# Turning the convolution's kernels onto time: TensorE transposes or transposing transfers

## The chip, the cores and the metric

The kernel runs on one core of one Trainium2 chip. The metric is the device time of one execution in microseconds (us): the median of three timed runs. Beside them stands one profiled execution, whose span runs from its first to its last instruction.

## The reference

Four layers are applied to `x` (2048 positions, 640 channels), each with a residual: attention, a convolution over positions, the same attention, the same convolution. Cut to what matters:

```python
def _A_ref(x, wqkv, wo):               # 32 heads of 20 channels
    q, k, v = split(x @ wqkv)
    return (softmax(q k^T * Dh ** -0.5) v) @ wo
def _B_ref(u, log_A_real, A_imag, C_real, C_imag, log_dt, D_skip):
    K = 2.0 * einsum("dn,dnl->dl", C, exp(A * dt * pos)).real    # one kernel of 2048 taps per channel
    y = irfft(rfft(K, 2 * L) * rfft(u^T, 2 * L), 2 * L)[:, :, :L]
    return y + u * D_skip
x = x + _A_ref(_layernorm(x), ...); x = x + _B_ref(_layernorm(x), ...)   # and both once more
```

## The kernel before, in words

During the first attention the kernels `K` (640 channels by 2048 taps) are computed beside it and stored in HBM as `kd`. They are needed as spectra. `ktransform` makes these from `kd` for both convolutions, once, while the first attention's output projection runs (`out_proj`). It takes the channels in five blocks of 128 (`b`). Each block goes through these steps:

- `load_kl(b)`: a 1 MB transfer on SP's queue brings `kl`, channels on partitions and 2048 taps along them.
- `by_time(b, h)`, two halves: TensorE turns eight groups of 128 taps (float32 transposes, four to one PSUM tile `pkt` of pool X). ScalarE writes the high float16 part `ktrh` (in the code `hi`) out of PSUM, scaled, and VectorE the low part `ktrl` (`lo`). The second half ends with `load_kl(b + 1)`.
- `first_stage(b, n)`, four of them: 24 float16 matmuls each with the constants `e1` on the parts, into two PSUM tiles `pkx` of pool X; ScalarE and VectorE copy one each to `x1` (in the trace `kx`).
- `turned(t, xt, h)`, four of them: 8 float32 transposes out of `x1` into two PSUM tiles `pkt` of pool X; one goes to `xt` by ScalarE and one by VectorE (`kxt`).
- `ends(t, xt, s, dst)`, four of them: 32 small matmuls `pkf`, four copies `kn`, two stores of 512 KB to `kha` or `khb`. It reads the whole of one `xt`.

`ktransform` is a generator. `out_proj` works through 16 rows of 30 matmuls each (`po`, 128x320 in float32 parts), 480 in all. It takes one step of the generator ahead of its first matmul and one more after every seven (`mm` and `weave`); what is left over runs after the last. Before the change there are 2 + 4 + 4 x 14 + 8 = 70 steps. `matmul` and `transpose` tie each matmul to the one before, so TensorE runs in just this order. Pool X has two PSUM tiles, pool M (for `po`) two, `kn` two per kind.

Each row of `out_proj` splits the row after next into parts: ScalarE writes `oh`, VectorE `ol`, of which there is one buffer; a transfer `otl` on SP's queue loads the next. After a row, the layer norm runs on VectorE and ScalarE (`u`, `uh`) and GpSimd (`ul`). SP issues its transfers in order: those of the constants (`e1s` first), of `otl`, `kl` and the stores of `kn`. The tile `late[1]` holds the last VectorE instruction of the attention; `hold` ties the first VectorE step of a block behind it, and later behind the last scaled copy of `turned`.

When `out_proj` is done, `ssm`, the convolution, begins with matmuls `psx` on `uh` and `ul`, and loads `eb` and the spectra `ka`, `kb`.

Of the kernel before, what the change touches and what calls it, by code (L numbers as in the profile page):

```python
# [11 lines left out]
F32 = mybir.dt.float32  # L12
F32R = mybir.dt.float32r
F16 = mybir.dt.float16
BF16 = mybir.dt.bfloat16
AF = mybir.ActivationFunctionType
ALU = mybir.AluOpType
# [4 lines left out]
P = 128  # L22
# [3 lines left out]
NCT = D // P  # L26
# [61 lines left out]
def mha_s4d_kernel(ctx, tc, x_in, wqkv, wo, lar, aim, cr, ci, ldt, dsk,  # L88
# [4 lines left out]
    def tie(made, before):  # L93

        if before is not None:
            tc.add_manual_dep(made.ins, before.name, mybir.DependencyInfo(
                mybir.DependencyClass.NoSync, mybir.DependencyReason.DATA), reason="order")
        return made.ins

    te = nc.tensor  # L100
    se, ve, ge, sy = (Ordered(e, plan, tie, e is nc.vector) for e in (nc.scalar, nc.vector, nc.gpsimd, nc.sync))
# [10 lines left out]
    def pst(pool, *a, **k):  # L112
        return ps_[pool].tile(*a, **k)
# [4 lines left out]
    kha = dram.tile([2 * NCT, P, 4, 4, P], F32, name="kha")  # L118
    khb = dram.tile([2 * NCT, P, 4, 4, P], F32, name="khb")
# [10 lines left out]
    ident = cp.tile([P, P], F32, name="ident")  # L130
# [5 lines left out]
    ksc = cp.tile([P, 2], F32, name="ksc")  # L136
# [52 lines left out]
    def chain(ins):  # L189
        last[0] = tie(ins, last[0])  # L190

    def matmul(*a, **k):
        chain(te.matmul(*a, **k))  # L193

    def transpose(*a, **k):
        chain(te.transpose(*a, **k))  # L196
# [1022 lines left out]
    def load_kl(b):  # L1219

        sy.dma_start(kl0[0], kd[b * P:b * P + P, :])
# [18 lines left out]
    def by_channel(x1, i2):  # L1240
        return x1[:, :, i2].rearrange("p c s g -> p s c g")

    def of_group(x1, g):
        return x1[:, :, :, :, g].rearrange("p c i s -> p (c i s)")

    def ktransform(e1):

        c = ExitStack()
        c2 = c.enter_context(tc.tile_pool(name="f2", bufs=2))
        kl, skip, f2, x1, hi, lo, *xts = kl0  # L1250
        hold = [late[1]]

        def by_time(b, h):

            if h == 0:
                tie(ve.tensor_add(kl[:, 0:1], kl[:, 0:1], skip[:, b:b + 1]), hold[0])
            klv = kl.rearrange("d (p i) -> d i p", i=NI)
            for i4 in (2 * h, 2 * h + 1):
                pt = pst("X", [P, 4, P], F32, tag="X", name="pkt")
                for i in range(4):  # L1260
                    transpose(pt[:, i, :], klv[:, 4 * i4 + i, :], ident)
                s4 = slice(4 * i4, 4 * i4 + 4)
                se.activation(hi[:, s4, :], pt, AF.Copy, scale=ksc[:, 0:1])
                ve.scalar_tensor_tensor(lo[:, s4, :], pt, ksc[:, 0:1], hi[:, s4, :], ALU.mult, ALU.subtract)
            if h and b + 1 < NCT:
                load_kl(b + 1)

        def first_stage(b, n):
            for i2 in (2 * n, 2 * n + 1):
                ps = pst("X", [P, 2, 2, P], F32, tag="X", name="pkx")  # L1270
                for i in range(2):
                    s = 2 * i2 + i
                    for r in range(2):
                        for n, (e, m) in enumerate(((0, hi), (0, lo), (1, hi))):
                            matmul(ps[:, r, i, :], e1[:, e, s, r, :], m[:, s, :], start=(n == 0), stop=(n == 2))
                (ve.tensor_copy if i2 % 2 else se.copy)(by_channel(x1, i2), ps.rearrange("p r i (c g) -> p (r i) c g", c=4))

        def block(b):

            def turned(t, xt, h):  # L1280
                for q in (2 * h, 2 * h + 1):
                    pt = pst("X", [P, 4, P], F32, tag="X", name="pkt")
                    for g in range(4):
                        transpose(pt[:, g, :], of_group(x1, 16 * t + 4 * q + g), ident)
                    if q % 2:
                        hold[0] = ve.tensor_scalar_mul(xt[:, q], pt, ksc[:, 1:2]).ins
                    else:
                        se.activation(xt[:, q], pt, AF.Copy, scale=ksc[:, 1:2])

            def ends(t, xt, s, dst):  # L1290
                px = [pst("F", [P, 512], F32, tag=f"F{ch}", name=f"pkf{ch}") for ch in range(4)]
                for ch in range(4):
                    rows = slice(32 * ch, 32 * ch + 32)
                    for g in range(4):
                        matmul(px[ch][32 * g:32 * g + 32, :].rearrange("p (q k) -> p q k", k=P), f2[rows, s, :],
                               xt[rows, :, g, :], start=True, stop=True, tile_position=(32 * ch, 32 * g))
                for h in range(2):
                    kn = c2.tile([P, 2, 4, P], F32, name=f"kn{s}")
                    for ch in range(2):
                        (se.copy if ch else ve.tensor_copy)(kn[:, ch], px[2 * h + ch].rearrange("p (q k) -> p q k", k=P))  # L1300
                    sy.dma_start(dst[2 * b + t][:, 2 * h:2 * h + 2], kn)
            steps = [(turned, 0, xts[0], 0), (turned, 0, xts[0], 1), (by_time, b + 1, 0), (ends, 0, xts[0], 0, kha),
                     (turned, 1, xts[1], 0), (ends, 0, xts[0], 1, khb), (turned, 1, xts[1], 1), (by_time, b + 1, 1),
                     (ends, 1, xts[1], 0, kha), (first_stage, b + 1, 0), (ends, 1, xts[1], 1, khb),
                     (first_stage, b + 1, 1), (first_stage, b + 1, 2), (first_stage, b + 1, 3)]
            for f, *a in steps:
                if f in (turned, ends) or b + 1 < NCT:
                    f(*a)
                    yield
        for h in range(2):  # L1310
            by_time(0, h)
            yield
        for n in range(4):
            first_stage(0, n)
            yield
        for b in range(NCT):
            yield from block(b)
        c.close()
# [329 lines left out]
    def seq(x, general):  # L1648

        stats = None  # L1650
        for n in range(0, len(parts), 2):
            with ExitStack() as c:
# [23 lines left out]
                with ExitStack() as c2:  # L1676
                    up2 = c2.enter_context(tc.tile_pool(name="up2", bufs=2 + n))

                    def ln(i0, m):
                        held = []  # L1680

                        def one(i):
                            if not held:
                                held.extend(ln_stats(lambda i: x[:, i0 + i, :], m))
                            mv, rs = held
                            ln_u(x, i0 + i, 1, (mv[:, i:i + 1, :], rs[:, i:i + 1]), uh, ul, up2, not general)
                        return [lambda i=i: one(i) for i in range(m)]
                    if general:
                        for i0 in range(0, NI, LG):
                            for f in ln(i0, LG):  # L1690
                                f()
                    else:
                        if n == 0:
                            filler[:] = ktransform(consts[0]), 0.0, False
                        out_proj(x, *tail, ln, load if early else None)
                        se.floor = None
# [97 lines left out]
```

## Time and profile before

| | |
|---|---|
| median of three runs | 2646.85 us (2645.38 to 2647.79) |
| span of the profiled execution | 2647.0 us |
| TensorE (PE) busy | 94% of the span |
| ScalarE (ACT) busy | 89% |
| VectorE (DVE) busy | 57% |
| GpSimd (POOL) busy | 30% |

The profile shows one execution. Its own time is its span, 2647.0 us; nothing around it is shown, and it stands 0.15 us from the median. The page gives busy times, but matmuls are pipelined, so the duration of one says less than the distance between the starts of two. The chain of waits follows the work back from the last instruction; there a group of matmuls appears with the time that it holds the chain.

### The profile page before, as it was taken

What the parts mean: (1) busy time and instruction counts of PE and PEld (TensorE: products, weight loads), DVE (VectorE), ACT (ScalarE), POOL (GpSimd) and SP (SyncE); (2) the same over time, 40 slices, a digit from 0 to 9 for tenths busy, and PEclk for the clock granted to TensorE, in tenths of its full rate; (3) what the DMA queues carried; (4) which work ended last, traced back from release to release, by engine and by line L of the source; (5) the groups of instructions that cost most, each with busy time, mean ns of one, the idle gap of its engine ahead of it and who ended that gap; (6) DMA issues with size and microseconds to landing.
All of it is one profiled execution on the core that took longest, in us unless ns stands there. A gap on an engine that the chain in (4) does not pass through costs nothing.

```text
span 2647.0 us, 118800 instructions
## 1 busy us (share of the span) xinstructions
PE 2492.4 (94%) x52388; PEld 1409.8 (53%) x52388; DVE 1519.5 (57%) x3430; ACT 2344.0 (89%) x2763; POOL 801.7 (30%) x1230
## 2 busy tenths in 40 slices
PE   6899999999999999899898999999999998999898
PEld 3444444454444444587896544454444443444898
DVE  7587777777765887577786323232232222143875
ACT  7899999999999999655665899999999999999574
POOL 1123333233323332111681122222222223222285
PEclk9999999999999999999999999999999999999999
DMA  6522222322222221654652111121121113222466
GB/s 206 189 53 77 68 74 62 82 65 63 61 54 59 53 63 38 234 206 163 213 173 64 47 53 50 51 60 45 45 66 39 50 34 87 71 66 61 137 190 184
DMA packets 188158, 241.99 MB, mean 91 GB/s; under 512 B 43504, under 2 KB 128816, under 8 KB 186224
## 3 DMA queue, kind: packets, MB, share of 16 engines
q1 hardware_dynamic: 151936, 188.28, 22.6%
q0 software_dynamic: 35696, 46.01, 7.4%
q8 instruction: 413, 6.77, 1.1%
q14 instruction: 113, 0.93, 0.1%
HBM read 158.16 MB, written 76.00 MB: 88 GB/s over the span
## 4 chain that ended last, share of the span: by engine, by line
ACT 59%; PE 20%; issue 10%; DVE 3%; DMA 2%; POOL 1%; SPq 0%; ACTq 0%; POOLq 0%; DVEq 0%
ACT pt L78 57%; PE psy L1430 3%; PE pa L903 2%; PE psv L1430 2%; PE po L193 2%; PE psx L1430 2%; PE S L868 2%; PE pst L1452 1%; PE pkx L193 1%; PE pv L586 1%; PE m L620 1%; PE pkt L196 1%; PE pq L773 1%; DMA kb<-khb 1%; DMA kop<-ks 1%
## 5 line engine op out<-in xcount | busy, mean ns | idle before, releaser
L78 ACT ACTIVATE pt<-S 128x1024 f32<-128x1024 f32 x2048 | 1927.7, 1033 | 27.9 <-PE S L868 15.5
L903 PE MATMUL pa<-pt,V 64*32 64x512 f32 x16384 | 1096.9, 589 | 1.4 <-DVE oc L78 1.4
L868 PE MATMUL S<-qop,kop 61*32 61x512 f16 x16384 | 877.2, 380 | 82.7 <-ACT pt L78 67.8
L868 PEld LDWEIGHTS <-kop 61*32 61x32 f16 x16384 | 366.9, 89 | 737.3 <-issue 619.2
L903 PEld LDWEIGHTS pa<-pt,V 64*32 64x32 f32 x16384 | 312.7, 106 | 72.0 <-issue 8.6
L78 POOL DMA_DIRECT2D dn<-oc x248 | 122.7, 501 | 574.2 <-DVE oc L78 574.1
L78 DVE TENSOR_SCALAR qc<-m 128x512 f32<-128x512 f32 (+1 forms) x68 | 46.8, 688 | 312.0 <-PE m L620 312.0
L78 POOL DMA_DIRECT2D db<-dn x248 | 125.4, 512 | 141.5 <-DMA dn<-dr 136.9
L78 POOL DMA_DIRECT2D ot<-oc x256 | 130.5, 517 | 88.4 <-DVE oc L78 55.5
L620 PE MATMUL m<-xl,wh 64*32 64x512 f16 x2560 | 143.8, 376 | 0.3 <-issue 0.3
L620 PE MATMUL m<-xh,wh 64*32 64x512 f16 x2560 | 144.1, 378 | 0.0
L620 PE MATMUL m<-xh,wl 64*32 64x512 f16 x2560 | 143.8, 377 | 0.0
L78 DVE COPY oc<-pa 128x512 f32<-128x512 f32 x64 | 44.2, 690 | 172.9 <-PE pa L903 168.9
L78 ACT COPY xt<-pst 128x1024 f16<-128x1024 f16 x80 | 81.3, 1016 | 60.8 <-PE pst L1452 60.8
L620 PEld LDWEIGHTS <-wh 64*32 64x32 f16 x5120 | 90.3, 93 | 73.3 <-issue 30.8
L78 POOL DMA_DIRECT2D dn<-dr x62 | 34.6, 558 | 287.3 <-DVE dr L78 248.6
L1480 POOL TENSOR_TENSOR kb<-t,kb 128x512 f32<-128x512 f32 x76 | 97.2, 1280 | 65.2 <-DVE t L78 40.8
L78 DVE TENSOR_SCALAR V<-m 128x160 f32<-128x160 f32 x64 | 20.7, 324 | 163.4 <-PE m L586 163.4
L78 DVE TENSOR_TENSOR kb<-ktab 128x512 f32<-128x512 f32 x160 | 106.2, 683 | 0.0
L586 PEld LDWEIGHTS <-xh 128*128 128x128 f16 x960 | 79.7, 98 | 46.7 <-issue 31.4
L1480 POOL TENSOR_TENSOR ka<-ka,kb 128x512 f32<-128x512 f32 x76 | 97.5, 1283 | 6.0
L337 PEld LDWEIGHTS m<-kb,ka 128*32 128x32 f32 x3840 | 60.8, 109 | 71.0 <-issue 52.4
(312 smaller groups left out, 3936.4 us busy)
## 6 DMA issues: line engine op xcount, KB each, us to landing
ka<-kha SPq DMA_DIRECT2D x80, 256.0 KB
kb<-khb SPq DMA_DIRECT2D x80, 256.0 KB
db<-dn POOLq DMA_DIRECT2D x248, 64.0 KB, 3.2
kop<-ks SPq DMA_DIRECT2D x176, 80.0 KB
kpw<-wd POOLq DMA_DIRECT2D x60, 192.0 KB, 3.9
qop<-qs SPq DMA_DIRECT2D x256, 40.0 KB
ot<-oc POOLq DMA_DIRECT2D x256, 40.0 KB, 3.0
kha<-kn SPq DMA_DIRECT2D x20, 512.0 KB
```

Source lines behind the costliest of these rows:

```text
L78: made = f(out, *a, **k)
L193: chain(te.matmul(*a, **k))
L196: chain(te.transpose(*a, **k))
L337: chain(te.matmul(ps[32 * j:32 * j + 32, c8, :], a[n][:, ch, :], b[n][:, dd, :], start=(n == 0), stop=(n == 2), tile_position=(0, 32 * j)))
L586: chain(te.matmul(ps[:, :n], a_[:, ct, sl], m[:, ct, :], start=(k == 0), stop=(k == 14)))
L620: chain(te.matmul(ps[r][32 * t:32 * t + 32, :], a_[rows, ct, 32 * u:32 * u + 32], m[rows, ct, 512 * v:512 * v + 512], start=(k == 0), stop ...
L773: te.matmul(pq, a_[:, ct, :], m[:, ct, sl], start=(n == 0), stop=(n == 14))
L868: chain(te.matmul(S[32 * t:32 * t + 32, 512 * r:512 * r + 512], kt_[rows, kc + 32 * t:kc + 32 * t + 32], qt[rows, :], start=True, stop=Tru ...
L903: chain(te.matmul(pa[r][32 * j:32 * j + 32, :], V[rows, kt, VP * h:VP * h + 32], pts[j // 2][rows, 512 * (j % 2):512 * (j % 2) + 512], sta ...
L1430: at("pe", te.matmul(*a, **k))
L1452: at("pe", te.transpose(pt[:, k, g, :], of_group(x1[k], 4 * q + g), id16))
L1480: at("pool", getattr(ge, f)(*a))
```

## The change

`by_time` no longer uses TensorE or PSUM. Out of `kl` as loaded it writes the two float16 parts with channels still on partitions, 1024 taps at a time: ScalarE the high part, VectorE the low part. They lie in `klp`, which is the memory of `xts[1]`, the second `kxt` tile, seen as float16. A new step `turn(b, h)` issues two transposing transfers on SP's queue, each of a 128x1024 float16 half (256 KB), from `klp` to `hi` and `lo`.

The order of steps is another too. `by_time` runs two blocks ahead, within `first_stage` of the next block, and `turn` one block ahead, at the start of a block. Neither counts as a step in a block. At the start, `by_time(0)`, `turn(0)`, `by_time(1)` and `first_stage(0)` run one after another. There are 4 + 2 + 4 + 4 x 12 + 8 = 66 steps.

```diff
         kl, skip, f2, x1, hi, lo, *xts = kl0
         hold = [late[1]]
+        spare = xts[1].rearrange("p a b k -> p (a b k)").bitcast(F16).rearrange("p (n i k) -> p n i k", n=2, k=P)
+        klp = [spare[:, n] for n in range(2)]
 
         def by_time(b, h):
 
             if h == 0:
                 tie(ve.tensor_add(kl[:, 0:1], kl[:, 0:1], skip[:, b:b + 1]), hold[0])
             klv = kl.rearrange("d (p i) -> d i p", i=NI)
-            for i4 in (2 * h, 2 * h + 1):
-                pt = pst("X", [P, 4, P], F32, tag="X", name="pkt")
-                for i in range(4):
-                    transpose(pt[:, i, :], klv[:, 4 * i4 + i, :], ident)
-                s4 = slice(4 * i4, 4 * i4 + 4)
-                se.activation(hi[:, s4, :], pt, AF.Copy, scale=ksc[:, 0:1])
-                ve.scalar_tensor_tensor(lo[:, s4, :], pt, ksc[:, 0:1], hi[:, s4, :], ALU.mult, ALU.subtract)
+            s8 = slice(8 * h, 8 * h + 8)
+            se.activation(klp[0][:, s8], klv[:, s8], AF.Copy, scale=ksc[:, 0:1])
+            ve.scalar_tensor_tensor(klp[1][:, s8], klv[:, s8], ksc[:, 0:1], klp[0][:, s8], ALU.mult, ALU.subtract)
             if h and b + 1 < NCT:
                 load_kl(b + 1)
+
+        def turn(b, h):
+
+            s8 = slice(8 * h, 8 * h + 8)
+            for a_, b_ in ((hi, klp[0]), (lo, klp[1])):
+                sy.dma_start_transpose(a_[:, s8], b_[:, s8].rearrange("d i p -> d (i p)"))
...
-            steps = [(turned, 0, xts[0], 0), (turned, 0, xts[0], 1), (by_time, b + 1, 0), (ends, 0, xts[0], 0, kha),
-                     (turned, 1, xts[1], 0), (ends, 0, xts[0], 1, khb), (turned, 1, xts[1], 1), (by_time, b + 1, 1),
-                     (ends, 1, xts[1], 0, kha), (first_stage, b + 1, 0), (ends, 1, xts[1], 1, khb),
-                     (first_stage, b + 1, 1), (first_stage, b + 1, 2), (first_stage, b + 1, 3)]
+            steps = [(turn, b + 1, 0), (turn, b + 1, 1), (turned, 0, xts[0], 0), (turned, 0, xts[0], 1),
+                     (ends, 0, xts[0], 0, kha), (turned, 1, xts[1], 0), (ends, 0, xts[0], 1, khb), (turned, 1, xts[1], 1),
+                     (ends, 1, xts[1], 0, kha), (first_stage, b + 1, 0), (ends, 1, xts[1], 1, khb), (by_time, b + 2, 0),
+                     (first_stage, b + 1, 1), (by_time, b + 2, 1), (first_stage, b + 1, 2), (first_stage, b + 1, 3)]
             for f, *a in steps:
-                if f in (turned, ends) or b + 1 < NCT:
+                if f in (turned, ends) or a[0] < NCT:
                     f(*a)
-                    yield
+                    if f is not turn and f is not by_time:
+                        yield
+        for f in (by_time, turn):
+            for h in range(2):
+                f(0, h)
+                yield
         for h in range(2):
-            by_time(0, h)
+            by_time(1, h)
             yield
```

## Rows read from the trace of the kernel before

**Rows 1.** The page: span, and busy us (share) xinstructions of each engine.
```profile
span 2647.0 us, 118800 instructions
PE 2492.4 (94%) x52388; PEld 1409.8 (53%) x52388; DVE 1519.5 (57%) x3430; ACT 2344.0 (89%) x2763; POOL 801.7 (30%) x1230
```
**Rows 2.** Windows: stretch, length, busy us (xinstructions) of PE, PEld, DVE, ACT, POOL; clock.
```profile
1089.00:1099.00 10.00, 5.99 (x44) 4.40 (x33) 9.30 (x14) 3.34 (x5) 2.52 (x5) 0.97 0.81 238
...
1142.00:1175.00 33.00, 32.66 (x387) 27.68 (x385) 24.43 (x50) 19.88 (x34) 5.65 (x4) 1.00 0.56 200
```
**Rows 3.** Groups of instructions, 1089 to 1262 us: busy, mean ns | idle before.
```profile
L78 DVE TENSOR_SCALAR kxt<-pkt,ksc 128x512 f32<-128x512 f32 x20 | 15.0, 748 | 7.6 <-PE pkt L196 7.5
L78 DVE SCALAR_TENSOR_TENSOR ktrl<-pkt,ksc,ktrh 128x512 f16<-128x512 f32 x20 | 14.5, 747 | 9.9 <-ACT ktrh L78 9.8
L78 DVE TENSOR_TENSOR ol<-otl,oh 128x640 fp32r<-128x640 f32 x15 | 12.2, 814 | 0.2
L78 ACT ACTIVATE ktrh<-pkt,ksc 128x512 f16<-128x512 f32 x20 | 13.1, 684 | 11.8 <-PE pkt L196 11.7
L196 PE MATMUL pkt<-ident,kl 128*128 128x128 f32 x80 | 12.2, 297 | 5.1 <-ACT kxt L78 3.5 <-issue 1.2 <-ACT oh L78 0.3
L78 ACT CAST uh<-u 128x640 f16<-128x640 f32 x15 | 10.7, 720 | 0.0
```
**Rows 4.** Timeline of PE around one group of transposes: start, us, instruction [idle before].
```profile
1147.58 1.14 PE L196 MATMUL pkt<-ident,kl 128*128 128x128 f32 x8 [0.34 <-ACT oh L78]
1148.48 1.12 PE L193 MATMUL po<-woh,ol 128*128 128x320 f32 x6
```
**Rows 5.** The chain that ended last, 1152 to 1157 us: start, us, what.
```profile
1152.91 1.03 PE po L193 x7
1153.94 1.07 PE pkf L193 x32
1155.01 1.23 PE po L193 x7
1156.24 0.89 PE pkt L196 x8
```
**Rows 6.** Timelines of PE and DVE at the start of the projection.
```profile
1091.70 1.58 PE L193 MATMUL po<-woh,ol 128*128 128x320 f32 x7
...
1099.02 0.26 PE L193 MATMUL pkx<-ktrh,e1s 128*128 128x128 f16 x1 [3.51 <-DVE ktrl L78]
...
1096.86 0.76 DVE L78 TENSOR_TENSOR ol<-otl,oh 128x640 fp32r<-128x640 f32 x1
```
**Rows 7.** Timeline of SP's queue at the start of the projection.
```profile
1089.72 2.62 SPq L78 DMA_DIRECT2D e1s<-in_c_e  x4
...
1094.80 0.38 SPq L78 DMA_DIRECT2D kl<-kd  x1
```
**Rows 8.** DMA: queue's packets, MB, share; traffic 1089 to 1262 us; one issue's landing.
```profile
q1 hardware_dynamic: 151936, 188.28, 22.6%
...
DMA packets 16675, 31.85 MB, mean 184 GB/s; under 512 B 1446, under 2 KB 10039, under 8 KB 16141
...
kd<-ko POOLq DMA_DIRECT2D x20, 256.0 KB, 3.3
```
**Rows 9.** Timelines of DVE and PE in the last block, where nothing parts the steps.
```profile
1245.43 0.75 DVE L78 TENSOR_SCALAR kxt<-pkt,ksc 128x512 f32<-128x512 f32 x1
...
1246.34 1.14 PE L193 MATMUL pkf<-kxt,f 32*32 32x512 f32 x32
```
**Rows 10.** Timeline of PE at the end of the projection, and one wait of PE.
```profile
1257.07 1.69 PE L193 MATMUL pkf<-kxt,f 32*32 32x512 f32 x32
...
1263.57 0.22 PE L1430 MATMUL psx<-uh,e1s 128*128 128x128 f16 x1 [2.03 <-DVE x L78]
...
PE psx L1430 <- DMA kb<-khb: 0.4, 1, 0.4
```
**Rows 11.** Waits of SP's queue, 1089 to 1262 us: us in total, times, longest.
```profile
SPq L78 <- DVE ol L78: 42.8, 10, 12.6
```

## The prediction, before the run

> **What bounds the kernel now.** I read the page first. Over the whole span TensorE is busy 94% and ScalarE 89% [rows 1], but the change touches only the output projection of the first attention, about 1089 to 1258 us, so these shares decide nothing. The windows come next. In a settled stretch of 33.00 us TensorE is busy 32.66, VectorE 24.43, ScalarE 19.88 [rows 2]; there TensorE is the bound, and work taken from it should shorten the stretch one for one. At the start it is not: in the ten microseconds from 1089 it is busy 5.99, VectorE 9.30. The grouped instructions then show the transposes of `kl`: 80 of them, 12.2 us busy, with 5.1 us of idle time right before them, 3.5 of it until ScalarE's `kxt` [rows 3]. As matmuls overlap, I price a group of eight by the distance of starts: from 1147.58 to the next `po` at 1148.48, 0.90 us [rows 4]. The chain shows the beat that the rest keeps: seven `po` take 1.03 us (0.147 each), an `ends` 1.07, the seven after it 1.23, a `turned` 0.89 [rows 5].
>
> **What the change removes from TensorE.** Ten groups of eight transposes go. The first two lie in the start, which is settled by itself below; the other eight are on TensorE's path: 8 x 0.90 = 7.2 us off. Of the idle time before them, the 1.2 us of "issue" goes with them. The 3.5 us until `kxt` I keep: ScalarE's copy was late there, and the next step, now `ends`, reads the same tile after the same seven `po`. What comes out of step with it is priced below.
>
> **ScalarE and VectorE.** Twenty `ktrh` of 0.684 and twenty `ktrl` of 0.747 us become ten each of twice the length, out of SBUF with a step of 64 bytes [rows 3]. No row has that shape. Scaled from 640 to 1024 elements, `uh` (0.720) gives 1.15 us and `ol` (0.814) 1.30; the pairs they replace cost 1.37 and 1.49. Were the step to double them, 10 x 1.15 and 10 x 1.30 us more would spread over some 150 us in which each engine has idle time [rows 2]. I take nothing for either, since TensorE's beat covers them; without that cover it is up to 1.2 us a half for whatever copy queues behind, `kx` or the adds of `po` first.
>
> **The start.** Before, the first `pkx` came at 1099.02, after 3.51 us of waiting for `ktrl` [rows 6], and by the order of steps 14 `po` lay ahead of it. Now it is the seventh step, and 42 lie ahead: 28 x 0.147 = 4.1 us of later work is done early. When can it start? `po` begins at 1091.70; row 0 has 30, to 1096.1. Row 1 needs `ol`, which ended at 1097.62 [rows 6]; with VectorE's two low parts in place of four shorter copies I put it 1 us later, 1098.6. Twelve more `po` end at 1100.4. The other side is the transfers. SP is through with the constants at 1094.80, when it issued `kl` [rows 7].
>
> No row shows a transposing transfer. A lower bound for the time it holds the queue is its bytes: 256 KB at the stretch's mean of 184 GB/s is 1.4 us. An upper one counts packets: the queue's 151936 packets took 22.6% of 16 engines' 2647.0 us, 63 ns each [rows 1, 8]; if each of the 1024 rows of 256 bytes (128 partitions by 8 groups) were a packet of its own, an engine has 64 of them, 4.0 us. I take 1.5 us, near the bytes, because the mean packet here is already a short one (1.2 KB). Landing adds about 2 us: a plain 256 KB transfer took 3.3 from issue to landing [rows 8].
>
> The first pair lands at 1095.2 + 2 x 1.5 + 2 = 1100.2, before TensorE asks. If `kl` for block 1 goes ahead of it, 1 MB at 184 GB/s puts 5.6 us in front: 1105.8. So the first `pkx` comes 1.4 to 6.8 us later than before. ScalarE is exposed here as well: `by_time(1)` waits for this `kl` and for `turn(0)` to have read `klp`, and `oh` and the copies `kx` queue behind it. I take +3.5 us, between the ends, since which goes first on SP is not to be read from the trace of before.
>
> **A settled block.** `turn(b + 1)` waits on SP for the last `first_stage` of the block before; behind it wait the stores of `kn` and `otl`, none of them due at once. Four transfers of 1.5 us follow. `turned(1, xts[1], 0)` then overwrites the memory they read, so its two copies wait for the third transfer. That is at 3 x 1.5 + 2 = 6.5 us. TensorE gets there after four stretches of `po`, two `turned`, one `ends` and the transposes themselves: 3 x 1.03 + 1.23 + 3 x 0.9 + 1.07 = 8.1 us. So it is hidden, with 1.6 us to spare; at 4.0 us a transfer it is not (first rival). `hi` and `lo` are not read until the first `first_stage`, over 5 us further on. `by_time(b + 2)` writes `klp` after the `ends` that read it; TensorE has passed that by then.
>
> The removed steps also parted `turned` from the `ends` that reads it, at eight places. Now seven `po`, 1.03 us, must cover VectorE's `kxt`, 0.748. The last block of before had this order already: `kxt` ran 1245.43 to 1246.18 and `pkf` followed at 1246.34 [rows 9]. I take 0.1 us a place, 0.8 in all; bounds are 0 and, with one other copy of 0.75 us ahead on VectorE and 0.2 of signalling, 0.75 + 0.75 + 0.2 - 1.03 = 0.67, times 8 = 5.4.
>
> **The end.** With 66 steps for 69 places the last `ends` runs ahead of the last 25 `po` and no longer after them, at 1257.07 [rows 10]. It is still TensorE's work. The convolution's start hangs on the last row's layer norm and casts (a wait of 2.03 us on VectorE) and hardly on `kb` (0.4) [rows 10]. The 1.1 us that moves before the end of `po` and the copies `kn` that leave VectorE's and ScalarE's way there cancel, to within 1 us either way: 0.
>
> **The sum.** -7.2 - 1.2 - 4.1 + 3.5 + 0.8 + 0 = -8.2 us. The profiled execution's 2647.0 becomes 2638.8, and as it is 0.15 from the median I forecast 2639. With all ends favourable it is -12.1 or so with the end's 1 us, 2635; with all unfavourable, +0.7, 2648.
>
> [...]
>
> **The rivals.**
>
> *Transfers go by the packet (slower).* At 4.0 us the third of a block is done at 12 + 2 = 14 us, and the copies of `turned(1)` wait 6 us, in four blocks: 24. At the start, the fourth lands at 1095.2 + 16 + 2 = 1113, about 6 us after the third `first_stage` wants it. 2639 + 30 = 2669. It decides from about 2.6 us a transfer, where 4 x (3 x 2.6 + 2 - 8.1) eats 7 us of the gain. For it speaks that 256-byte rows are short; against it, that the packets of this queue are mostly small too and still move 184 GB/s [rows 8].
>
> *SP stands in the way (slower).* SP waits for `ol` ten times, the longest 12.6 us [rows 11]. If `turn` is queued behind such an `otl`, it starts that much late, and 12.6 - 1.6 = 11 us a block are lost, 44 at most; half of that is 2639 + 22 = 2661. Against it: these are waits with nothing else due.
>
> *The waits take the gain (no change).* 0.67 us at each of eight places and the start at +6.8: 2639 + 4.6 + 3.3 = 2647. For it speaks that the 3.5 us until `kxt` already show ScalarE late at just these places [rows 3].
>
> *More than forecast.* The start at +1.4 and the 3.5 us until `kxt` gone, because ScalarE has shorter work: 2647 - 12.1 - 3.5 = 2631.
>
> **How the numbers follow.** Chances: forecast 0.52 (its own range 2634 to 2644), more than forecast 0.14, no change 0.16, by the packet 0.13, SP in the way 0.05. 0.2% is 5.3 us, about what a measurement of this kernel can tell from no change; faster means below 2641.6. Of the forecast's 0.52 some 0.08 lie above that. Faster: 0.44 + 0.14 + 0.02 of the third rival = 0.60. Same: 0.08 + 0.14 = 0.22. Slower: 0.13 + 0.05 = 0.18. The range is 2630 to 2660: it holds all of the middle, most of the low case, and the milder part of the two slow ones, since a transfer of 3 us would give about 2650.
>
> **What would show it.** TensorE's group `pkt<-ident,kl` must be gone, and the time from one block's first `turned` to the next's be shorter by about 2 us. Transposing transfers should follow each other on SP within 1.5 us or so; if TensorE's waits list `pkf` or `pkt` behind `kxt`, and `kxt` behind a transfer, the first rival holds. The first `pkx` at 1100 to 1106 decides the start. The forecast is wrong if TensorE's idle time in this stretch grows by more than the 8 us that its work shrinks.

## The result and the profile after

The changed kernel is slower: 2659.70 us, the median of five runs (2654.4 to 2661.8), against 2646.42 us for the kernel before on the same chip (2644.36 to 2647.79, five runs). The ratio is 1.0049, 95% interval 1.0037 to 1.0061, some 13 us. Forecast were 2639 us and "faster"; the time lies just inside the range of 2630 to 2660, on its wrong side.

The page of the changed kernel begins as follows; the lines answer to [rows 1].

```profile
span 2659.9 us, 118664 instructions
PE 2491.8 (94%) x52308; PEld 1406.1 (53%) x52308; DVE 1524.6 (57%) x3420; ACT 2350.9 (88%) x2753; POOL 800.5 (30%) x1230
```

TensorE has 80 instructions less and is busy only 0.6 us less: that is the first hint. All further times are taken from the projection, from the end of the attention's last `pa` to the end of the last `po`, because the attention before it ends some us earlier or later from one profiled run to the next. These are the windows of that stretch in the kernel before and then in the changed one (stretch, length, busy PE, PEld, DVE, ACT, POOL, granted clock, DMA share, GB/s).

```profile
1089.58:1257.14 167.56, 156.49 (x1818) 131.16 (x1824) 122.74 (x266) 92.09 (x152) 25.05 (x23) 0.98 0.51 179
```
```profile
1091.86:1272.14 180.28, 156.25 (x1766) 127.50 (x1766) 130.06 (x258) 99.55 (x144) 24.77 (x22) 0.94 0.68 205
```

The projection is 12.7 us longer, and TensorE's idle time grows by as much: 167.56 - 156.49 = 11.1 us before, 180.28 - 156.25 = 24.0 after. That is the sign which the prediction had named for being wrong, idle time that grows by more than 8 us. The busy time should have fallen by those 8 us and stayed, at a granted clock of 0.94 against 0.98. One thing is not alike in the two stretches: before, the last `ends` (1.1 us of TensorE) ran after the last `po` [rows 10] and lies outside; now it lies inside. The waits of TensorE from 1089 to 1273 us say what it waited for (total, times, longest; before, the longest row was 3.5).

```profile
PE pkx L193 <- ACT kx L78: 5.8, 3, 3.2
PE pkx L193 <- DMA ktrl<-kxt: 4.1, 1, 4.1
PE m L888 <- DVE oc L78: 4.0, 1, 4.0
PE po L193 <- DVE x L78: 3.7, 3, 3.1
PE pkf L193 <- ACT kxt L78: 3.3, 3, 2.6
PE pkx L193 <- DVE kx L78: 2.5, 3, 1.3
```

Rows two and three and most of row four lie in the first 25 us; the others, in the blocks. Next, the groups of instructions of the changed kernel, which answer to [rows 3]: the splits of `kl` (the buffer `klp` goes by `kxt` in the trace).

```profile
L78 ACT ACTIVATE kxt<-kl,ksc 128x1024 f16<-128x1024 f32 x10 | 20.1, 2030 | 6.5 <-DVE kl L78 6.5
L78 DVE SCALAR_TENSOR_TENSOR kxt<-kl,ksc,kxt 128x1024 f16<-128x1024 f32 x10 | 19.6, 1962 | 12.4 <-ACT kxt L78 10.0 <-DMA ktrl<-kxt 2.4
```

ScalarE's takes 2.03 us, VectorE's 1.96; the estimates were 1.15 and 1.30. What that does is seen in a settled block. These are the timelines of ScalarE, VectorE and TensorE around 1150 us.

```profile
1147.41 0.71 ACT L78 CAST uh<-u 128x640 f16<-128x640 f32 x1
1148.03 0.57 ACT L78 COPY kn<-pkf 128x512 f32<-128x512 f32 x1
1148.51 2.01 ACT L78 ACTIVATE kxt<-kl,ksc 128x1024 f16<-128x1024 f32 x1
1150.42 0.57 ACT L78 COPY kx<-pkx 128x512 f32<-128x512 f32 x1
...
1150.55 1.95 DVE L78 SCALAR_TENSOR_TENSOR kxt<-kl,ksc,kxt 128x1024 f16<-128x1024 f32 x1 [3.46 <-ACT kxt L78]
1152.41 0.69 DVE L78 COPY kx<-pkx 128x512 f32<-128x512 f32 x1
...
1146.50 0.22 PE L193 MATMUL pkx<-ktrh,e1s 128*128 128x128 f16 x1
...
1151.04 0.22 PE L193 MATMUL pkx<-ktrh,e1s 128*128 128x128 f16 x1 [3.24 <-ACT kx L78]
...
1153.15 0.26 PE L193 MATMUL pkx<-ktrh,e1s 128*128 128x128 f16 x1 [1.29 <-DVE kx L78]
```

TensorE finished two tiles `pkx` by 1146.7, which fills pool X. The copy `kx` that would empty the first stands on ScalarE behind layer norm work, a `kn` and the split, and starts at 1150.42. VectorE's low part has to wait for ScalarE's high part (3.46 us of idle time), and VectorE's `kx` stands behind it. So TensorE waits twice, 3.24 and 1.29 us, and for the work behind the waits the granted clock is lower:

```profile
1152.50:1156.00 3.50, 2.85 (x18) 2.85 (x18) 3.46 (x6) 1.51 (x3) 2.39 (x1) 0.52 0.66 119
```

That window has a granted clock of 0.52; in the settled stretch of [rows 2] it was 1.00. The `po` there start 0.27 us apart and not 0.147.

The start is the other place. SP's queue first, then VectorE and TensorE, all in the changed kernel; [rows 6, 7] are their counterparts.

```profile
1095.33 1.38 SPq L1270 DMA_TRANSPOSE ktrh<-kxt  x1
1096.76 2.75 SPq L78 DMA_DIRECT2D e1s<-in_c_e  x4
...
1102.58 0.33 SPq L78 DMA_DIRECT2D kl<-kd  x1
...
1104.10 3.52 SPq L1270 DMA_TRANSPOSE ktrl<-kxt  x1
1107.66 3.18 SPq L1270 DMA_TRANSPOSE ktrh<-kxt  x1
1110.88 1.31 SPq L1270 DMA_TRANSPOSE ktrl<-kxt  x1
...
1095.34 1.93 DVE L78 SCALAR_TENSOR_TENSOR kxt<-kl,ksc,kxt 128x1024 f16<-128x1024 f32 x1 [2.77 <-ACT kxt L78]
1097.18 0.68 DVE L78 TENSOR_TENSOR oc<-oc,pa 128x512 f32<-128x512 f32 x1
...
1102.46 3.38 DVE L78 RECIPROCAL db<-db 128x128 f32<-128x128 f32 x4
...
1097.92 1.98 PE L888 MATMUL m<-oc,dsel 128*128 128x512 f32 x2 [3.95 <-DVE oc L78]
1106.24 0.99 PE L193 MATMUL po<-woh,ol 128*128 128x320 f32 x5 [3.09 <-DVE x L78]
...
1108.36 0.23 PE L193 MATMUL pkx<-ktrh,e1s 128*128 128x128 f16 x1
1112.68 0.27 PE L193 MATMUL pkx<-ktrl,e1s 128*128 128x128 f16 x1 [4.09 <-DMA ktrl<-kxt]
```

The first transfer waits for a split and holds up the constants `e1s` (4.9 us after the last `pa`, before 0.1); the load of `kl` for block 1 goes ahead of the other three, and the second and third hold the queue for over 3 us each. On VectorE the low part, which waits for ScalarE first, stands ahead of the `oc` additions that the attention's last matmul `m` needs: 3.95 us. The second low part and the attention's reciprocals, late behind it, stand ahead of the add of `x`: 3.09. The first low part lands 4.09 us after TensorE asked. In settled blocks the same transfers are short: of the twelve for blocks 2 to 4, eleven hold the queue for 1.23 to 1.40 us and one for 2.63. A row of them, and the queue's packets in the whole run (before, 151936 [rows 8]):

```profile
1150.54 1.24 SPq L1270 DMA_TRANSPOSE ktrh<-kxt  x1
...
q1 hardware_dynamic: 173056, 193.53, 23.7%
```

### The profile page after: what moved, and what is told of

It reads as the page before. It is cut to its first block, busy times and chain, and to the rows that moved or that the text cites. A ratio compares the mean times of both kernels' runs of the same rounds, so it can differ in the third digit from the quotient of the medians.

```text
span 2659.9 us, 118664 instructions
## 1 busy us (share of the span) xinstructions
PE 2491.8 (94%) x52308; PEld 1406.1 (53%) x52308; DVE 1524.6 (57%) x3420; ACT 2350.9 (88%) x2753; POOL 800.5 (30%) x1230
## 3 DMA queue, kind: packets, MB, share of 16 engines
q1 hardware_dynamic: 173056, 193.53, 23.7%
## 4 chain that ended last, share of the span: by engine, by line
ACT 58%; PE 19%; issue 10%; DVE 4%; DMA 3%; POOL 1%; SPq 0%; ACTq 0%; POOLq 0%; DVEq 0%
ACT pt L78 56%; PE psy L1439 3%; PE pa L903 2%; PE psv L1439 2%; PE psx L1439 2%; PE po L193 2%; PE S L868 2%; PE pst L1461 1%; DMA kop<-ks 1%; PE pv L586 1%; PE pkf L193 1%; PE pkx L193 1%; PE pq L773 1%; PE m L620 1%; DVE x L78 1%
## 5 line engine op out<-in xcount | busy, mean ns | idle before, releaser
L78 ACT ACTIVATE pt<-S 128x1024 f32<-128x1024 f32 x2048 | 1927.8, 1033 | 29.9 <-PE S L868 17.8
```

The lines of the kernel that those rows point to most:

```text
L78: made = f(out, *a, **k)
```

## The experiments

Each kernel is the changed one with the edit shown. "Projection" is its length in the profiled run as above, and idle is TensorE's in it.

| kernel | ratio to before (95%) | projection, us | idle, us |
|---|---|---|---|
| before | 1 | 167.6 | 11.1 |
| changed | 1.0049 (1.0037 to 1.0061) | 180.3 | 24.0 |
| contig | 1.0013 (1.0004 to 1.0022) | 172.8 | 17.8 |
| no_turn | 1.0044 (1.0031 to 1.0057) | 180.8 | 24.4 |
| start_pe | 1.0031 (1.0020 to 1.0043) | 175.1 | 17.4 |
| quarters | 1.0052 (1.0039 to 1.0065) | 179.7 | 24.3 |
| contig_pe | 1.0002 (0.9993 to 1.0011) | 166.3 | 11.8 |
| no_split | 0.9994 (0.9985 to 1.0003) | 162.1 | 9.5 |
| write_step | 1.0179 (1.0165 to 1.0193) | 215.9 | 53.6 |
| late_one | 1.0090 (1.0075 to 1.0105) | 186.6 | 30.2 |
| start_kl | 1.0055 (1.0041 to 1.0069) | 181.8 | 25.1 |
| pool_split | 1.0071 (1.0057 to 1.0085) | 188.6 | 26.7 |

**contig: the splits read neighbours.**

```diff
-            klv = kl.rearrange("d (p i) -> d i p", i=NI)
+            klv = kl.rearrange("d (i p) -> d i p", i=NI)
```

> The split reads kl with its taps side by side instead of with a step of 64 bytes; same instructions, same order, so the taps are in the wrong order and the output is not the reference's. Theory A (the 64-byte step doubles the splits to 2.03 us on ScalarE and 1.96 on VectorE, and the copies kx and kxt queue behind them): the splits fall to about 1.15 and 1.3 us, TensorE's waits for kx (8.3 us) and kxt (3.3) shrink by more than half, time 2648 to 2653. Rival B (the transposing transfers crowd the DMA queue): the splits may get shorter but the time stays at 2657 to 2662.

The groups of its trace, the order of instructions being the same on every engine:

```profile
L78 DVE SCALAR_TENSOR_TENSOR kxt<-kl,ksc,kxt 128x1024 f16<-128x1024 f32 x10 | 12.8, 1281 | 8.7 <-ACT kxt L78 5.6 <-DMA ktrl<-kxt 2.9
L78 ACT ACTIVATE kxt<-kl,ksc 128x1024 f16<-128x1024 f32 x10 | 11.3, 1150 | 7.6 <-DVE kl L78 7.6
```

1.15 and 1.28 us, what the forecast had worked out. So the step of 64 bytes costs 0.88 us a split on ScalarE and 0.68 on VectorE, and with it gone the projection is 7.5 us shorter. The waits for `kx` fall from 8.3 to 3.0 us, as theory A had it; those for `kxt` stay at 3.3, so the splits' length is not their reason. The start keeps its wait: `ktrl` still landed 5.5 us after it was wanted.

**no_turn: no transfers for blocks 1 to 4.**

```diff
-                if f in (turned, ends) or a[0] < NCT:
+                if f in (turned, ends) or a[0] < NCT and f is not turn:
```

> The transposing transfers of blocks 1 to 4 are left out, those of block 0 stay; hi and lo keep block 0's taps, so the output is not the reference's. Theory A (splits and their order on ScalarE and VectorE): the splits and the waits behind them stay, time 2655 to 2661. Rival B (transfers crowd the queue, or the copies wait for them to have read): the projection gets 8 to 12 us shorter, time 2646 to 2651.

The time stays that of the changed kernel, within the intervals. In settled blocks the transposing transfers cost nothing that shows, 180.3 us of projection with them and 180.8 without; the prediction's first rival is out there.

**start_pe: block 0 turned by TensorE as before.** `by_pe` is the old `by_time`.

```diff
-        for f in (by_time, turn):
-            for h in range(2):
-                f(0, h)
-                yield
         for h in range(2):
-            by_time(1, h)
+            by_pe(h)
             yield
         for n in range(4):
+            if n in (1, 2):
+                by_time(1, n - 1)
             first_stage(0, n)
```

> Block 0 is turned by TensorE as before the change, the split of block 1 then runs within the first stages of block 0; all other blocks as changed. Theory: the start costs about 8 us more than forecast, because SP's first transposing transfer stands ahead of the constants e1s, and kl and otl ahead of the second. Expected: first pkx 9 to 11 us after the end of the attention's matmuls (20.8 in the changed kernel, 9.4 before), time 2650 to 2654. If the start's loss is caught up later anyway: 2657 to 2661.

5.2 us of projection come back. The first `pkx` is again 9.45 us after the last `pa` (before 9.44, changed 20.8), and the waits of `m` and of the first adds are again about those of before (0.5 and 0.6, before 0.5 each). The waits on `kx` stay, as its rows show:

```profile
PE pkx L193 <- ACT kx L78: 7.1, 5, 3.1
PE pkx L193 <- DVE kx L78: 2.8, 3, 1.4
```

**quarters: splits of 512 taps, one behind each first stage.**

```diff
-            s8 = slice(8 * h, 8 * h + 8)
...
+            for q in (2 * h, 2 * h + 1) if n is None else (n,):
+                s4 = slice(4 * q, 4 * q + 4)
...
+                     ... (by_time, b + 2, 0, 0),
+                     (first_stage, b + 1, 1), (by_time, b + 2, 0, 1), (first_stage, b + 1, 2), (by_time, b + 2, 1, 2),
+                     (first_stage, b + 1, 3), (by_time, b + 2, 1, 3)]
```

> The splits of blocks 1 to 4 run in four quarters (512 taps), each behind the copies of a first stage and not ahead of them; work and transfers unchanged, the start as in the changed kernel. Theory A: what costs the settled blocks is not the splits' length as such but that copies kx wait behind a split of 2.0 us on ScalarE and the next one on VectorE; quarters of about 1.0 us behind the copies take back 6 to 10 us: 2650 to 2654. Rival B (transfers): 2657 to 2662. Rival C (the splits' total on ScalarE and VectorE): no change either, 2657 to 2662, with the quarters at half the length and the waits spread.

Nothing is won. In the first settled block ScalarE's timeline shows that most pieces did not come between the copies:

```profile
1144.51 0.57 ACT L78 COPY kx<-pkx 128x512 f32<-128x512 f32 x1
1144.97 3.30 ACT L78 ACTIVATE kxt<-kl,ksc 128x512 f16<-128x512 f32 x3
1148.18 0.71 ACT L78 CAST uh<-u 128x640 f16<-128x640 f32 x1
1148.79 0.59 ACT L78 COPY kx<-pkx 128x512 f32<-128x512 f32 x1
```

Three ran back to back, 3.30 us, and then the `kx`. In the two later blocks the pieces stood three and one, and two and two, ahead of the next two `kx`. So this run doesn't say what it would cost if each piece stood behind a copy. The time is what rival C forecast, and the waits for ScalarE's `kx` are spread somewhat (5.2 us in four, changed 5.8 in three); the run doesn't rule C out. Rival B is out by no_turn.

**contig_pe: both edits.** Those of contig and start_pe.

> Both single edits that won time back, in one kernel: the splits read neighbouring elements (the taps come out in another order), and block 0 is turned by TensorE with the splits of block 1 behind its first stages. Theory (two separate costs, the length of the splits in the blocks and the order of the start): the savings add, projection 180.3 - 7.5 - 5.2 = 167.6 us, time 2643 to 2645, ratio to before 0.998 to 0.9995. Rival (one cost seen twice, the copies that queue behind the splits, which the start shows too): no better than the better of the two alone, projection 172 to 173 us, time 2648, ratio 1.0005 to 1.002.

They add: 180.3 - 7.5 - 5.2 = 167.6 was expected, 166.3 measured. The ratio, 1.0002, lies above the theory's range and just below the rival's; the projection decides for two separate costs. With both gone the time is that of the kernel before: the change gains nothing that can be measured.

**no_split: neither splits nor transfers for blocks 1 to 4, block 0 by TensorE.**

```diff
-            se.activation(klp[0][:, s8], klv[:, s8], AF.Copy, scale=ksc[:, 0:1])
-            ve.scalar_tensor_tensor(klp[1][:, s8], klv[:, s8], ksc[:, 0:1], klp[0][:, s8], ALU.mult, ALU.subtract)
...
-                if f in (turned, ends) or a[0] < NCT:
+                if f in (turned, ends) or f is not turn and a[0] < NCT:
```

> Block 0 is turned by TensorE as in the kernel before; for blocks 1 to 4 the splits and the transfers are left out, so they use block 0's parts again. What is left of the change is that TensorE's transposes of four blocks are gone. Theory (the splits alone took the gain of the blocks): the forecast's own terms without a start, 167.6 - 7.2 - 1.2 + 0.8 = 160 us of projection, time 2638 to 2640, ratio 0.997 to 0.998. Rival (ScalarE's and VectorE's other copies would have been late without the splits too, so TensorE only waits longer): projection 164 to 167 us, time 2643 to 2646, ratio 0.9985 to 1.000.

The projection came to 162.1 us, between the theory's 160 and the rival's 164. The time fell by 0.06%, which is in the rival's range and is not told from nothing. The rival's reason fails, though: TensorE does not wait longer, its idle time is 9.5 us against 11.1. Two of its longer waits, beside the 3.5 us for the first `ktrl`, and the windows of this run and of start_pe:

```profile
PE pkf L193 <- ACT kxt L78: 2.4, 1, 2.4
PE pkx L193 <- ACT kx L78: 2.0, 1, 2.0
...
1084.99:1247.08 162.09, 152.58 (x1781) 126.09 (x1782) 114.32 (x252) 83.27 (x138) 23.52 (x22) 0.97 0.56 199
1085.00:1260.07 175.07, 157.72 (x1782) 129.82 (x1782) 128.82 (x260) 98.34 (x146) 24.15 (x22) 0.94 0.66 208
```

With no split at all one wait of 2.0 us for a ScalarE copy is left, and the late `kxt` that before fell on `pkt` (3.5 in all) falls on `pkf`. What is missing to 160 us is no added waiting. 1.1 us is the last `ends`, which now lies inside the projection, and the granted clock is 0.97 where it was 0.98; over 162 us that is an estimated 1.6 us. start_pe runs the same matmuls, and the splits make it wait 7.9 us more (17.4 against 9.5) and work 5.1 us longer (157.72 against 152.58) at 0.94. From the projection's end on, no_split needs 1.9 us more than the kernel before (2638.9 - 1247.1 = 1391.8 against 2647.0 - 1257.1 = 1389.9); no_turn and the changed kernel, whose ends are alike, differ by more (1391.6 and 1387.8), so nothing follows from that.

The blocks show where the splits cost. From one block's first `turned` to the next's the changed kernel takes 33.6, 34.5, 30.6 and 27.8 us, no_split 29.5, 30.5, 27.2 and 27.8. The first three stretches hold splits, the last has transfers and no split: where the splits end, the loss ends.

**write_step: the splits read in the order of memory and step in their writes.**

```diff
+            kls, kph, kpl = (t[:, s8].rearrange("d i p -> d p i") for t in (klv, *klp))
-            se.activation(klp[0][:, s8], klv[:, s8], ...)
+            se.activation(kph, kls, AF.Copy, scale=ksc[:, 0:1])
-            ve.scalar_tensor_tensor(klp[1][:, s8], klv[:, s8], ..., klp[0][:, s8], ...)
+            ve.scalar_tensor_tensor(kpl, kls, ksc[:, 0:1], kph, ALU.mult, ALU.subtract)
```

> The splits go through kl in the order of its memory, eight neighbours at a time, and it is the writes to klp that step (256 bytes); same values as in the changed kernel, nothing else differs. Theory A (the step of 64 bytes on the reading side makes the splits long): ScalarE's split 1.15 us, VectorE's 1.28 as with neighbouring reads, projection about 173 us, time 2648 to 2650. Theory B (any step on either side costs): both stay near 2.0 us or over, VectorE's more because its second operand steps as well, time 2658 to 2662.

```profile
L78 ACT ACTIVATE kxt<-kl,ksc 128x1024 f16<-128x1024 f32 x10 | 48.5, 4946 | 8.3 <-DVE kl L78 8.3
L78 DVE SCALAR_TENSOR_TENSOR kxt<-kl,ksc,kxt 128x1024 f16<-128x1024 f32 x10 | 48.3, 4832 | 25.6 <-ACT kxt L78 25.2 <-ACT lt L78 0.4
```

Both forecasts missed. With two-byte writes 256 bytes apart, and on VectorE a second operand read at that step, a split took 4.9 us on ScalarE and 4.8 on VectorE, far more than with the stepped reads. So the run can't test what theory A says of the reads; contig does. Theory B had the direction and not the size. As a test of the length it is useful: 2.9 us more on each split make the projection 35.6 us longer than in the changed kernel.

**late_one and start_kl: the start taken apart.** The first moves only block 1's splits behind the first `pkx`, the second issues block 1's `kl` behind block 0's transfers.

```diff
-        for h in range(2):
-            by_time(1, h)
-            yield
         for n in range(4):
+            if n in (1, 2):
+                by_time(1, n - 1)
             first_stage(0, n)
```
```diff
-            if h and b + 1 < NCT:
+            if h and 0 < b < NCT - 1:
                 load_kl(b + 1)
...
+            if b == 0 and h:
+                load_kl(1)
```

> As the changed kernel, but block 1's two splits stand behind the first and the second first stage of block 0 and not ahead of them, so 14 fewer po come before the first pkx; block 0 is still turned by transfers. Theory A (the order of the steps and the splits queued in front set the start): first pkx 14 x 0.147 = 2 us and a split earlier, 16 to 18 us after the attention's last pa in place of 20.8, time 2655 to 2657. Theory B (the landing of block 0's transfers sets it, at about 20 us after that pa): first pkx within 1 us of 20.8, a longer wait for ktrh or ktrl, time 2658 to 2661.

> As the changed kernel, but the load of kl for block 1 (1 MB) is issued behind block 0's four transfers, not ahead of three of them. Theory (that load stands in their way on SP's queue and keeps their data waiting): block 0's last ktrl lands 4 to 6 us earlier than the 20.8 us after the attention's last pa that it took, first pkx at 15 to 17 us, time 2653 to 2656. Rival (the transfers are late because the splits that feed them are, behind the copies of the attention's end): landing within 1.5 us of before, time 2658 to 2662, or later still, since block 1's splits now wait for their kl.

One row of late_one's waits, and from start_kl a row of TensorE and one of SP's queue:

```profile
PE pkx L193 <- DMA ktrl<-kxt: 9.2, 1, 9.2
```
```profile
1105.71 0.22 PE L193 MATMUL pkx<-ktrl,e1s 128*128 128x128 f16 x1 [1.09 <-DMA ktrl<-kxt]
...
1098.61 4.52 SPq L1270 DMA_TRANSPOSE ktrl<-kxt  x1
```

In late_one TensorE reached the first `pkx` at 1099.37 and stood for 9.2 us: the landing sets the start, as theory B had it, and the 14 `po` that were put ahead in the changed kernel had hidden some of it. The price was larger than either theory had, 25 us over the kernel before; the projection shows 19.0 of it, and where the rest arose was not followed up. In start_kl `ktrl` landed 17.8 us after the last `pa` and not 20.8: the load did stand in the way, for 3 us of the 4 to 6 expected. It is not what held the first `ktrl` on the queue, though: that took 4.52 us here, with the constants and an `otl` ahead of it and no `kl`. And the time is no shorter. Block 1's `kl` now landed at 1112.4, its two splits on ScalarE (3.94 us, from 1112.50) came ahead of the third `kx`, and the waits on ScalarE's `kx` rose from 5.8 to 9.0 us.

**pool_split: GpSimd makes the splits, block 0 by TensorE.** The edit on top of start_pe:

```diff
-            se.activation(klp[0][:, s8], klv[:, s8], AF.Copy, scale=ksc[:, 0:1])
-            ve.scalar_tensor_tensor(klp[1][:, s8], klv[:, s8], ksc[:, 0:1], klp[0][:, s8], ALU.mult, ALU.subtract)
+            if h == 0:
+                ge.tensor_scalar_mul(kl, kl, ksc[:, 0:1])
+            ge.tensor_copy(klp[0][:, s8], klv[:, s8])
+            ge.tensor_sub(klp[1][:, s8], klv[:, s8], klp[0][:, s8])
```

> Block 0 is turned by TensorE as in the kernel before; for blocks 1 to 4 GpSimd makes the splits (scales kl in place, copies it to float16, subtracts), and ScalarE and VectorE make none. GpSimd has the time: 26 of 186 us are busy there in the changed kernel. Theory (the copies kx queue behind the splits on ScalarE and VectorE; take the splits off these two and that wait goes): kx waits fall from 9.9 us with the splits there to the 2.0 us that stayed without any splits, projection 162 to 165 us against 175.1, time 2641 to 2645, ratio 0.9985 to 1.000. Rival (GpSimd's five instructions of about 1.5 ns or more an element, some 12 us a block, end so late that the transfers, and the copies of turned that overwrite their source, wait): projection 170 us or more, time 2649 or more, ratio over 1.0015.

```profile
1106.18 5.45 POOL L1262 TENSOR_SCALAR kl<-kl,ksc 128x2048 f32<-128x2048 f32 x1 [7.67 <-DVE x L78]
1111.70 3.88 POOL L1263 CAST kxt<-kl 128x1024 f16<-128x1024 f32 x2
1115.53 5.32 POOL L1264 TENSOR_TENSOR kxt<-kl,kxt 128x1024 f16<-128x1024 f32 x2
...
1108.12 2.46 DVE L78 TENSOR_TENSOR ol<-otl,oh 128x640 fp32r<-128x640 f32 x1 [0.16 <-PE po L193]
...
1127.93 0.75 DVE L78 TENSOR_SCALAR kxt<-pkt,ksc 128x512 f32<-128x512 f32 x1 [9.68 <-DMA ktrh<-kxt]
```

The rival held. GpSimd needs 14.7 us a block, 1.9 to 2.7 ns an element, where the rival's estimate was some 12 us at 1.5 ns or more (before, `ul` took 1.41 us for 640 elements, 2.2 ns each), and is through at 1120.9; the transfers follow, and VectorE's `kxt`, which overwrites what they read, waits 9.68 us for them (TensorE 8.7 behind it). That is the wait that the prediction had worked out for slow transfers, reached through a slow split. Of TensorE's waits for `kx`, 5.5 us stay, where the theory had 2.0.

## Why the prediction was wrong

Along the chain before, no_split, start_pe, changed, each step is one term:

| term | forecast, us | measured, us of projection |
|---|---|---|
| blocks without transposes: -7.2 - 1.2 + 0.8 | -7.6 | 162.1 - 167.6 = -5.5 |
| splits on ScalarE and VectorE | 0 | 175.1 - 162.1 = +13.0 |
| start: -4.1 + 3.5 | -0.6 | 180.3 - 175.1 = +5.2 |
| sum | -8.2 | +12.7 |

These are differences of single profiles. In the first row the last `ends`, 1.1 us, moves into the measured stretch, so -6.5 is the forecast to compare with -5.5. The ratios give the same steps as -0.06, +0.37 and +0.18% of 2646 us: -2, +10 and +5 us, uncertain by some 2, 4 and 4.

- **The step that failed** is "I take nothing for either, since TensorE's beat covers them". The split's length was wrong by 0.9 and 0.7 us, and the place mattered as much: busy shares of 24.43 and 19.88 in 33.00 us [rows 2] say that an engine has time, not that its next copy does. The text had the mechanism in its next clause (copies `kx` queue behind) and priced it at nothing. What the runs show in its place is +13.0 us: 7.9 us more waiting, and 5.1 us by which the same matmuls take longer, at a granted clock of 0.94 against 0.97 (start_pe against no_split). For the clock the prediction had no term. Of the 13.0 us, 175.1 - 166.3 = 8.8 go with the step in the reads; 4.2 remain with splits of the forecast's length, and the ratios, 1.0002 and 0.9994, do not tell those 4.2 from nothing.
- **A doubled cost was named and dropped.** "Were the step to double them" is nearly what happened: 1.8 times on ScalarE (2.03 us against 1.15 in contig), 1.5 on VectorE (1.96 against 1.28).
- **The start** was taken as +3.5, at most +6.8. The first `pkx` that reads `ktrl` came 20.8 us after the last `pa` and not 9.44, 11.4 later; by the projection, the net of +5.2 with the 4.1 of early work kept makes the term +9.3. Not seen were that the transfer holds up `e1s`, that VectorE's low parts stand ahead of the attention's last `oc` and of the `x` adds, and that of the three transfers behind `kl` two hold the queue for over 3 us. What each of these costs by itself no run shows.
- **The removal** was right, in size to within 1 us: for blocks 1 to 4 the transposes `pkt<-ident,kl` are gone in no_split and the projection is 5.5 us shorter, where 6.5 was due. The adjacency of `turned` and `ends`, +0.8, cost little: in no_split `pkf` waits 2.4 once, where before `pkt` waited 3.5.
- **The transfers** were right: 1.24 us each on an open queue, where 1.5 was taken, and without cost in the settled blocks (no_turn). The upper bound had the packets right and their price wrong: 20 transfers add 173056 - 151936 = 21120 packets, 1056 each, and 1.24 us on 16 engines is an estimated 19 ns a packet, where 63 was taken. By the bytes, 256 KB in 1.24 us of the queue is 211 GB/s, where the lower bound had the stretch's mean of 184.
- **The end** can't be told from the 0 that was taken: the last `pkf` now starts at 1267.03, ahead of the last `po`, and from the projection's end on the run takes 2659.9 - 1272.1 = 1387.8 us against 1389.9, but no_turn, with the same end, takes 1391.6.

What stays open: whether splits of 1.15 us still cost the 4.2 us that the profiles show, and how much of it would go if they stood behind the copies. No run put them there. With this order of steps the change can't be expected to beat the kernel before by a margin that shows: without any split and transfer the ratio is 0.9994 (0.9985 to 1.0003).

## What to carry to other kernels

Work moved from the bound engine to half-idle ones is priced by its longest instruction and by what stands behind that in the queue: here a copy that empties one of two PSUM tiles stood there, and one split of 2.01 us left the bound engine waiting 3.24 us, whatever the busy shares said. Read the granted clock behind a wait too: here it was 0.52 behind two of them, and over the projection the same matmuls took 5.1 us longer, at 0.94 against 0.97, on top of 7.9 us of waiting (start_pe against no_split). When a copy out of PSUM becomes one out of SBUF, write down its step in bytes before scaling a duration from another row: at 64 bytes ScalarE's took 2.03 us here, 1.15 between neighbours. Where a stage begins, list what each queue still owes the stage before: this change put its first instructions ahead of three such debts.

## What was not expected of the hardware

- Reading 1024 float32 at a step of 64 bytes took ScalarE 2.03 us against 1.15 for neighbours, VectorE 1.96 against 1.28. Writing float16 at a step of 256 bytes took 4.9 and 4.8, on VectorE with one operand read at that step too.
- A transposing transfer of 128 x 1024 float16 came to 1056 packets (21120 more in the queue for 20 of them). It held SP's queue for 1.24 us in a settled block, for 3.52 behind a 1 MB load at the start, and for 4.52 behind other transfers without that load (start_kl).
- While GpSimd made its first splits, an `ol` on VectorE took 2.46 us (at 1108.12 in pool_split); the projection's fifteen took 1.11 on the mean, where [rows 3] have 0.81.
